# Scores of the first attention stage as float32 products of unsplit keys and queries

## The chip, the cores and the metric

The kernel runs on one core of a Trainium2 chip. TensorE (PE) multiplies, VectorE (DVE), ScalarE (ACT) and GpSimd (POOL) do the elementwise work, SyncE (SP) issues nearly all of the loads. The metric is the device time of one execution in microseconds (us). Before the change, three runs gave 691.86 (median), 690.34 and 691.96 us.

## The reference

Three blocks in a row, all in float32:

```
attention: B=2, H=8, S=768, D=64; key k is kept for query i if k < n_global (8) or 0 <= i-k < n_local (96)
  scores = q k^T / 8 - slope_h * distance;  softmax over the kept keys;  times v
swiglu (1536 tokens x 512): xn = rmsnorm(x);  (silu(xn w_gate) * (xn w_val)) w_out,  inner width 1536
top-1 of 8 experts: y = gate * relu(xe w1[e]) w2[e],  512 -> 1024 -> 512
```

## The kernel before, in words

The 1536 tokens are cut into six **stages** of two 128-row tiles (`SIZES`). A stage's attention is done for four **pairs** of heads (`hp`), so there are 24 groups, numbered `gi` = 4 * stage + pair, of two **units** each (one 128-row tile of queries). Below, (g, t) is unit t of group g; groups 0 to 3 are stage 0, and (4, 0) is the first unit of stage 1.

A unit goes through `scores` (PE products into two PSUM banks, one a head; then on DVE one instruction per head that adds the bias table and takes the row extreme, L492; then the exponential on ACT, L496), `turn` (four PE transposes, L507, copied out by ACT, L515) and `values` (PE products with v, L536; on DVE a reciprocal and the normalised rows into the tiles `part`, L543 to L546). These run up to three units apart. After the last pair of a stage, `tail` normalises its rows (L360 to L374), turns them (L381), and the stage's swiglu products can start (L704, tile `pg`).

PE's products run in the 4-byte format fp32r. The kernel splits their operands in an fp32r copy (the high part) and the rest that the copy leaves out. For the scores, the loads (L202) put a head's 64 dimensions twice on the 128 rows; `prep` makes the high part of the keys on ACT (L429), replaces the lower 64 rows by the rest (L432), makes the high part of the queries (L437 on DVE in the first four groups, L441 on ACT later) and their rest on DVE (L442). One head of a unit is then two fp32r products over 128 rows (L485). For the windowed stages, POOL copies the 32 global keys (`kg`) and the rows of neighbouring tiles into `kt` and `vx` (`pcopy`, L399).

SP loads the first three pairs into tiles of `part` ahead of everything else, five loads a pair (two halves of the keys, two of the queries, one for v). Only then it reads the flag that selects the fast path, and issues the first three swiglu weight loads (`raw`, 512 KB each, L295) and the next pairs. Weights arrive as pairs of words that DVE converts (tile `cv`, L310 to L319). A scheduler sets the order on each engine from the dependencies and its own time model; each engine then runs its list in order, so an instruction that waits holds up all that stand behind it.

Of the kernel before, what the change touches and what calls it, by code (L numbers as in the profile page):

```python
# [8 lines left out]
F32 = mybir.dt.float32  # L9
# [4 lines left out]
ACTF = mybir.ActivationFunctionType  # L14
ALU = mybir.AluOpType
# [4 lines left out]
P = 128  # L20
B, H, S, D = 2, 8, 768, 64
# [3 lines left out]
NP = H // 2  # L25
TT = NT // P
# [19 lines left out]
def kernel(  # L46
# [15 lines left out]
):  # L62
    nc = tc.nc
    slope = [2.0 ** (-(h + 1)) for h in range(H)]
    NFP, LATE = 3, 8
    XT = "ccccss"
    RING = "ccceewweec"
    FIRST = [0, 1, 1, 1, 1]
# [49 lines left out]
        out=nval, in0=nneg, scalar=4294967296.0, in1=nf[:, :, 0], op0=ALU.mult, op1=ALU.add  # L118
# [66 lines left out]
    qT = [q[b].rearrange("h d s -> (h d) s") for b in range(B)]  # L185
# [4 lines left out]
    def rows_of(vn):  # L190
        n = vn.shape[1] // VW
        return vn[:, 0:n * VW].rearrange("p (t c) -> p t c", c=VW)

    def load_pair(st, hp, kn, qn, vn):
# [4 lines left out]
        hd = slice(P * hp, P * (hp + 1))  # L199
        for x, src in ((kn[:, 0:2 * nk * P], kT[b][hd, k0:k0 + nk * P]), (qn[:, 0:2 * nt * P], qT[b][hd, t0 * P:(t0 + nt) * P])):  # L200
# [62 lines left out]
    def body(is_fast):  # L263
# [126 lines left out]

        def fast_attention(pool):
            kg = pool.tile([P, NP, 2, GW], F32R, name="kg")
            vg = pool.tile([P, P], F32, name="vg")
            groups = []
            loaded = list(first_pairs)

            def pcopy(o, i):
                src_ = i.bitcast(F32) if i.dtype == F32R else i
                nc.gpsimd.tensor_scalar(out=o, in0=src_, scalar1=1.0, scalar2=0.0, op0=ALU.mult, op1=ALU.add)  # L399

            def prep(gi):
# [3 lines left out]
                n = nt * P  # L405
                kn, qn, vn = loaded.pop(0)
                vn = rows_of(vn)
                nc.gpsimd.memset(vn[:, i0:nt + 1, 0:VW:VW - 1], 1.0)
                nxt = range(NFP, NFP + 2) if gi == 0 else range(gi + 2, gi + 3) if gi >= NFP else ()
                for gn in nxt:  # L410
                    if gn >= len(order):
# [34 lines left out]
                gr = slice(GW * hp, GW * (hp + 1))  # L446
                if t0 == 0:
                    pcopy(kg[:, hp], kt[:, :, OW + 1, 0:GW])
                    pcopy(vg[gr, :], vn[0:GW, 1, 1:P + 1])

                f = 1 if t0 >= 2 else 3 - t0
                nw = nt + 1 - f
                if nw > 0:
                    pcopy(kt[:, :, f - 1:nt, GW:], kt[:, :, OW + f - 1:OW + nt, GW:])
                    pcopy(kt[:, :, f - 1:nt, 0:GW], kg[:, hp].unsqueeze(2).to_broadcast([P, 2, nw, GW]))
                    pcopy(vx[:, f - 1:nt, :], vn[:, f - 1:nt, :])
                    pcopy(vx[0:GW, f - 1:nt, 1:P + 1], vg[gr, :].unsqueeze(1).to_broadcast([GW, nw, P]))
                mx = pool.tile([P, ST, 2], F32, tag="mx", bufs=3, name="mx")
# [4 lines left out]
            def scores(g, t):  # L463
# [12 lines left out]
                for j, a in ((0, 0), (0, 1), (1, 0), (1, 1)):  # L476
# [81 lines left out]
            n = hold = 0  # L558
# [740 lines left out]
```

## Time and profile before

| what | value |
|---|---|
| runs, median (lowest to highest) | 691.86 us (690.34 to 691.96) |
| profiled execution: own time / span | 690.83 / 689.1 us |
| mean granted TensorE clock | 0.953 of full |
| busy: PE, DVE, ACT, POOL | 637.0, 456.8, 324.6, 338.6 us |
| PE weight loads busy | 574.1 us |
| first score product / first swiglu product | 12.01 / 76.54 us |
| last score product | 168.8 us |

The profiled execution is about 1 us below the median of the runs. PE is busy for 92% of the span, but not evenly: the page's 40 slices show the granted clock at 6, 7 and 5 tenths in the second to fourth slice (17 to 69 us), where attention alone runs, and at 9 nearly everywhere later. From 76.5 us on swiglu products fill the gaps. After attention has ended, the rest is long chains of products. Fp32r shows as f32 in PE's rows.

### The profile page before, as it was taken

Reading aid. Unit: us, or ns where it says so; the run is one execution under the profiler, and the core shown is the slowest. Engines: PE = TensorE matmul, PEld = TensorE weight load, DVE = VectorE, ACT = ScalarE, POOL = GpSimd, SP = SyncE. Lnnn points to the kernel's source line nnn. Section 1 sums busy time; section 2 is a strip of 40 time slices with the busy share of each in tenths; the row PEclk is TensorE's granted clock in tenths of the full one; section 3 lists DMA queues with packets and bytes.
Section 4 is the critical chain, followed back from the end, with each engine's and each line's share of the span. In section 5 each row is a group of like instructions: output and inputs, shape, how many; then the busy total and the mean of one; then the engine's idle time right before and its main releaser. Section 6 shows DMA issues by size and latency. Waiting matters only on the chain. (4 is left out here: it accounts for less than half of the span.)

```text
span 689.1 us, 11953 instructions
## 1 busy us (share of the span) xinstructions
PE 637.0 (92%) x4214; PEld 574.1 (83%) x4215; DVE 456.8 (66%) x1276; ACT 324.6 (47%) x631; POOL 338.6 (49%) x355
## 2 busy tenths in 40 slices
PE   6888998899998899999989999899989899999992
PEld 3677987899997788999889999797678798998891
DVE  6788799987589998225549999952356444555410
ACT  3685777867554543113632211241455545564420
POOL 2577547663254554113332332552777677667401
PEclk9675899999999999999999999999999999999997
DMA  6977447641034444000440120131578776667200
GB/s 182 235 193 185 107 127 180 176 132 35 1 119 125 127 130 145 1 1 6 163 138 14 50 62 32 49 120 63 167 241 242 192 251 206 201 195 228 82 12 28
DMA packets 57290, 85.16 MB, mean 124 GB/s; under 512 B 6655, under 2 KB 39423, under 8 KB 57216
## 3 DMA queue, kind: packets, MB, share of 16 engines
q1 hardware_dynamic: 54272, 76.91, 38.5%
q0 software_dynamic: 2944, 7.35, 3.2%
q8 instruction: 36, 0.59, 0.4%
q14 instruction: 38, 0.31, 0.2%
HBM read 77.91 MB, written 7.39 MB: 124 GB/s over the span
## 5 line engine op out<-in xcount | busy, mean ns | idle before, releaser
L704 PE MATMUL pg<-xn,gv 128*128 128x256 f32 x1728 | 229.0, 286 | 7.0 <-DVE hf L717 3.6
L704 PEld LDWEIGHTS pg<-xn,gv 128*128 128x128 f32 x1728 | 219.1, 192 | 13.8 <-DVE hf L717 4.9
L891 POOL TENSOR_TENSOR ew<-rawe,ew 128x512 fp32r<-128x512 f32 x64 | 100.8, 1590 | 48.2 <-ACT ew L885 46.4
L722 POOL TENSOR_TENSOR hid<-hf,hid 128x256 fp32r<-128x256 f32 x72 | 59.0, 824 | 119.9 <-ACT hid L721 119.6
L741 PE MATMUL po<-ow,hid 128*128 128x512 f32 x432 | 112.2, 399 | 1.5 <-DVE hf L717 1.2
L888 DVE TENSOR_TENSOR ew<-rawe,ew 128x512 fp32r<-128x512 f32 x64 | 65.4, 1027 | 68.2 <-ACT ew L885 67.5
L885 ACT ACTIVATE ew<-rawe 128x1024 fp32r<-128x1024 f32 x64 | 66.7, 1060 | 65.8 <-DMA rawe<-in_moe_w_dram 53.8
L945 PE MATMUL py<-ew,eh 128*128 128x512 f32 x384 | 91.2, 395 | 0.9 <-DVE eh L1012 0.9
L741 PEld LDWEIGHTS po<-ow,hid 128*128 128x128 f32 x432 | 77.4, 189 | 17.4 <-POOL hid L722 1.5
L967 PE MATMUL ph<-xs,ew 128*128 128x256 f32 x672 | 84.0, 283 | 3.6 <-ACT yo L951 2.7
L945 PEld LDWEIGHTS py<-ew,eh 128*128 128x128 f32 x384 | 71.4, 188 | 17.6 <-DVE eh L1012 1.5
L967 PEld LDWEIGHTS ph<-xs,ew 128*128 128x128 f32 x672 | 81.7, 189 | 4.9 <-ACT yo L951 2.9
L721 ACT ACTIVATE hid<-hf 128x256 fp32r<-128x256 f32 x72 | 29.8, 415 | 82.3 <-DVE hf L717 82.2
L774 DVE CUSTOM_DVE_ANT_0 jk<-part,rgb 128x256 bf16<-128x256 f32 x128 | 59.4, 507 | 0.0
L485 PE MATMUL sp<-kt,qt 128*128 128x256 f32 (+1 forms) x192 | 47.2, 351 | 12.0 <-DVE mx L492 5.6
L496 ACT ACTIVATE pr<-pr,mx 128x256 f32<-128x256 f32 (+1 forms) x96 | 44.5, 484 | 19.5 <-DVE mx L492 17.8
L327 POOL TENSOR_TENSOR gv<-cv,gv 128x512 fp32r<-128x512 f32 x24 | 32.8, 1370 | 34.4 <-ACT gv L326 31.8
L485 PEld LDWEIGHTS sp<-kt,qt 128*128 128x128 f32 x192 | 34.2, 227 | 18.0 <-DVE mx L492 5.8
L712 ACT ACTIVATE th<-pg 128x256 f32<-128x256 f32 x72 | 26.8, 376 | 44.1 <-PE pg L704 42.7
L713 DVE SCALAR_TENSOR_TENSOR th<-th,pg 128x256 f32<-128x256 f32 x72 | 29.6, 414 | 26.8 <-ACT th L712 26.8
L432 POOL TENSOR_TENSOR kt<-kn,kt 64x768 fp32r<-64x768 f32 (+1 forms) x21 | 38.0, 1811 | 8.8 <-issue 4.0
L316 DVE SCALAR_TENSOR_TENSOR cv<-raw,cv 128x512 uint32<-128x512 uint32 x36 | 35.8, 997 | 0.5
(174 smaller groups left out, 898.2 us busy)
## 6 DMA issues: line engine op xcount, KB each, us to landing
rawe<-in_moe_w_dram SPq DMA_DIRECT2D x64, 512.0 KB, 4.1
raw<-in_moe_w_gate_dram SPq DMA_DIRECT2D x12, 512.0 KB, 4.1
raw<-in_moe_w_val_dram SPq DMA_DIRECT2D x12, 512.0 KB, 3.7
raw<-in_moe_w_out_dram SPq DMA_DIRECT2D x12, 512.0 KB, 3.6
kn<-in_k_dram SPq DMA_DIRECT2D x32, 192.0 KB, 3.6
qn<-in_q_dram SPq DMA_DIRECT2D x42, 128.0 KB, 3.5
vn<-in_v_dram SPq DMA_DIRECT2D x16, 192.0 KB, 3.0
x1d<-part SPq DMA_DIRECT2D x12, 256.0 KB, 2.1
```

The source lines that it names most:

```text
L432: lo_eng[kq[0]].tensor_tensor(out=ks[D:P], in0=src[D:P], in1=ks[D:P].bitcast(F32), op=ALU.subtract)
L485: mm = nc.tensor.matmul(out=o, lhsT=qt[:, j, a, t * P:(t + 1) * P], rhs=rhs, start=(a == 0), stop=(a == 1))
L496: pin["act"] = nc.scalar.activation(out=pr[:, j, 0:n], in_=pr[:, j, 0:n], func=ACTF.Exp, bias=mx[:, t, j:j + 1], scale=-1.0,)
L704: nc.tensor.matmul(out=pg[:, 0:n_], lhsT=gv[:, i, a, kk, :], rhs=x[st][:, kk, :], start=(n == 0), stop=(n == 3 * KD - 1),)
L722: nc.gpsimd.tensor_tensor(out=hh[:, 1], in0=hf, in1=hh[:, 0].bitcast(F32), op=ALU.subtract)
L741: nc.tensor.matmul(out=po, lhsT=hid[mi][:, a, t * P:(t + 1) * P], rhs=ow[:, c, :], start=(mi == 0 and n == 0), stop=(mi == len(ms) - 1 and ...
L774: nc.vector.tensor_tensor_reduce(out=jk, in0=part[i0 + t][:, h * 256:(h + 1) * 256], in1=rgb[h][:, e, :], scale=1.0, scalar=0.0, op0=ALU.m ...
L885: cp = nc.scalar.activation(out=t[:, 0], in_=raw, func=ACTF.Copy)
L888: nc.vector.tensor_tensor(out=t[:, 1, 0:NDV], in0=raw[:, 0:NDV], in1=t[:, 0, 0:NDV].bitcast(F32), op=ALU.subtract)
L891: nc.gpsimd.tensor_tensor(out=t[:, 1, NDV:], in0=raw[:, NDV:], in1=t[:, 0, NDV:].bitcast(F32), op=ALU.subtract)
L945: last_mm["py"] = nc.tensor.matmul(out=py, lhsT=hid(m, a, j), rhs=w2t[m // 2][:, c, (m % 2) * DM:(m % 2 + 1) * DM], start=(n == 0), stop=( ...
L967: nc.tensor.matmul(out=ph[:, 0:CAP], lhsT=w1t[kk][:, a, m * P:(m + 1) * P], rhs=x[:, kk, :], start=(n == 0), stop=(n == 3 * KD - 1),)
```

## The change

For groups below `NRAWG` = 4, that is all four pairs of stage 0, keys and queries are loaded once: head 0 on rows 0 to 63, head 1 on rows 64 to 127. ACT scales the queries in place, and one head of a unit is one float32 product over its 64 rows. Four pairs instead of three are loaded ahead (`NFP`), three loads each, in two tiles of `part`. The ones beside v are set before the loads. As no split keys of stage 0 exist any more, the global keys come by two extra loads (`kgn`, 128-byte pieces), and ACT and POOL split them at group 2.

```diff
-    NFP, LATE = 3, 8
+    NFP, LATE = 4, 8
+    NRAWG = 4
...
+        if is_raw(st, hp):
+            nc.sync.dma_start(out=kn[:, 0:nk * P], in_=kT[b][hd, k0:k0 + nk * P])
+            nc.sync.dma_start(out=qn[:, 0:nt * P], in_=qT[b][hd, t0 * P:(t0 + nt) * P])
+            nc.sync.dma_start(out=rows_of(vn)[:, i0:i0 + nk, 1:P + 1], ...)
+            return kn, qn, vn
...
-    first_pairs = [load_pair(*order[i], *part[TT - 3 * (i + 1):TT - 3 * i]) for i in range(NFP)]
+    for i in range(NFP):
+        kq_, vn_ = part[TT - 2 * i - 2], part[TT - 2 * i - 1]
+        nc.gpsimd.memset(rows_of(vn_)[:, 1:3, 0:VW:VW - 1], 1.0)
+        first_pairs.append(load_pair(*order[i], kq_[:, 0:STAGE], kq_[:, STAGE:2 * STAGE], vn_))
...
+                if gi == 0:
+                    kg0 = kT[0].rearrange("(h d) s -> d h s", d=D)[:, :, 0:GW]
+                    for r in range(2):
+                        nc.sync.dma_start(out=kgn[D * r:D * (r + 1)].rearrange("d a j s -> d (a j) s"), in_=kg0)
+                if gi == 2:
+                    nc.scalar.activation(out=kg, in_=kgn, func=ACTF.Copy)
+                    nc.gpsimd.tensor_tensor(out=kg[D:P], in0=kgn[D:P], in1=kg[D:P].bitcast(F32), op=ALU.subtract)
...
+                if raw_:
+                    qs = qn[:, 0:n]
+                    nc.scalar.activation(out=qs, in_=qs, func=ACTF.Copy, scale=0.125 / slope[2 * hp])
+                    values_windows()
+                    groups.append((st, t0, hp, qs, (kn, kgr), vn, vx, mx))
+                    return
...
+                    for j in range(2):
+                        r = slice(D * j, D * (j + 1))
+                        lq = qt[r, t * P:(t + 1) * P]
+                        if t0 == 0:
+                            mm = nc.tensor.matmul(out=sp[j][:, 0:n], lhsT=lq, rhs=kn[r, 0:n], start=True, stop=True)
```

The scheduler makes new lists. On ACT, the first instructions behind the branch were the high keys of pairs 0, 1 and 2 (`part_120`, `part_117`, `part_114`):

```order
L429 ACTIVATE kt<-part_120 128x2x256
L429 ACTIVATE kt<-part_117 128x2x256
L496 ACTIVATE pr<-pr,mx 128x128 x2
L429 ACTIVATE kt<-part_114 128x2x256
L496 ACTIVATE pr<-pr,mx 128x256
```

Now they are the scalings of the queries of pairs 1, 2, 3 and, last, 0 (`part_119`, `part_117`, `part_115`, `part_121`):

```order
L470 ACTIVATE part_119<-part_119 128x256
L470 ACTIVATE part_117<-part_117 128x256
L470 ACTIVATE part_115<-part_115 128x256
L470 ACTIVATE part_121<-part_121 128x256
L558 ACTIVATE pr<-pr,mx 128x128 x2
L558 ACTIVATE pr<-pr,mx 128x256
L483 ACTIVATE kt<-kn 128x2x384
```

Pair 0's queries stand behind the last loaded pair's. On DVE, the row extremes of unit (1, 0) (`tab_145`, `half_165`) and of unit (1, 1) (`tabL`, `half_167`) had one weight conversion between them, and the queries of pair 3 (`qn`) behind them:

```order
L492 ISA pr,mx<-sp,tab_145 128x128
L492 ISA mx 128x1
L492 ISA pr,mx<-sp,half_165 128x128
L492 ISA mx 128x1
L310 TENSOR_SCALAR cv<-cv 128x512
L313 TENSOR_SCALAR cv<-cv 128x512
L316 SCALAR_TENSOR_TENSOR cv<-raw,cv 128x512
L492 ISA pr,mx<-sp,tabL 128x256
L492 ISA mx 128x1
L492 ISA pr,mx<-sp,half_167 128x256
L492 ISA mx 128x1
L437 TENSOR_SCALAR qt<-qn 128x2x256
```

Now, from the second head of (1, 0) on (`half_166`), the rests of the queries of pairs 4 and 5 (L496) stand there:

```order
L554 ISA pr,mx<-sp,half_166 128x128
L554 ISA mx 128x1
L496 SCALAR_TENSOR_TENSOR qt<-qn,qt 128x2x256
L333 SCALAR_TENSOR_TENSOR cv<-raw,cv 128x512
L554 ISA pr,mx<-sp,tabL 128x256
L554 ISA mx 128x1
L336 SCALAR_TENSOR_TENSOR cv<-raw,cv 128x512
L496 SCALAR_TENSOR_TENSOR qt<-qn,qt 128x2x256
L554 ISA pr,mx<-sp,half_168 128x256
L554 ISA mx 128x1
```

Both heads of (1, 1) now stand behind a load of a later stage. On SP, the list behind the branch is now this; before, pair 3 stood where pair 4 (the first `kn`, `qn`, `vn`) stands now, and pair 4 where pair 5 stands, with the weights all three ahead of them:

```order
L312 DMA raw<-in_moe_w_gate_dram 128x4x256
L312 DMA raw<-in_moe_w_val_dram 128x4x256
L215 DMA kn<-in_k_dram 64x2x384
L312 DMA raw<-in_moe_w_out_dram 128x1024
L215 DMA kn<-in_k_dram 64x2x384
L215 DMA qn<-in_q_dram 64x2x256 x2
L219 DMA vn<-in_v_dram 128x3x128
L215 DMA kn<-in_k_dram 64x2x384 x2
L215 DMA qn<-in_q_dram 64x2x256
L235 DMA gB<-in_moe_rms_g_dram 128x512
L215 DMA qn<-in_q_dram 64x2x256
L219 DMA vn<-in_v_dram 128x3x128
```

Pair 5's loads moved forward, the `kgn` loads follow two and five places behind. The first swiglu product stands behind the same number of units as before on PE (60 transposes and 56 value products in either list).

## Rows read from the trace of the kernel before

**Rows 1.** Windows: stretch; length, busy us (count) of PE, PEld, DVE, ACT, POOL; clock, DMA, GB/s

```profile
24.00:42.00 18.00, 16.27 (x68) 13.94 (x67) 14.26 (x46) 12.93 (x28) 14.12 (x16) 0.53 0.81 198
42.00:51.00 9.00, 6.49 (x52) 5.68 (x50) 8.77 (x29) 7.76 (x17) 6.54 (x9) 1.00 0.83 218
51.00:74.50 23.50, 19.63 (x85) 17.96 (x86) 18.62 (x55) 13.72 (x28) 17.06 (x22) 0.51 0.69 171
74.50:170.00 95.50, 89.39 (x702) 84.88 (x702) 85.80 (x287) 74.27 (x163) 54.99 (x83) 0.98 0.47 128
170.00:560.00 390.00, 371.78 (x2492) 336.79 (x2492) 260.27 (x717) 150.56 (x286) 173.64 (x158) 0.99 0.33 103
```

**Rows 2.** Timeline of PE: start, us, what, count, idle time before and its releaser

```profile
12.01 0.66 PE L485 MATMUL sp<-kt,qt 128*128 128x128 f32 x4 [2.10 <-DVE kt L432]
...
33.37 0.80 PE L485 MATMUL sp<-kt,qt 128*128 128x256 f32 x2 [0.91 <-POOL kt L399]
...
51.21 1.11 PE L485 MATMUL sp<-kt,qt 128*128 128x256 f32 x4 [1.51 <-POOL kt L399]
...
76.54 0.61 PE L704 MATMUL pg<-xn,gv 128*128 128x256 f32 x3
...
77.58 1.91 PE L704 MATMUL pg<-xn,gv 128*128 128x256 f32 x14
```

**Rows 3.** Timeline of SP's queue: start, us of issuing, load, count

```profile
1.77 1.37 SPq L202 DMA_DIRECT2D part<-in_k_dram  x2
...
10.94 0.59 SPq L206 DMA_DIRECT2D part<-in_v_dram  x1
12.61 0.38 SPq L295 DMA_DIRECT2D raw<-in_moe_w_gate_dram  x1
...
22.33 0.60 SPq L206 DMA_DIRECT2D vn<-in_v_dram  x1
```

**Rows 4.** DMA view, 0 to 14 us: load, count, KB each, median us to landing

```profile
part<-in_q_dram SPq DMA_DIRECT2D x6, 128.0 KB, 3.0
```

**Rows 5.** Timeline of DVE up to the first unit of stage 1

```profile
4.88 0.17 DVE L112 CAST nf<-nraw 128x4 f32<-128x4 int32 x1 [2.33 <-DMA nraw<-in_n_local_dram]
...
10.55 0.69 DVE L442 SCALAR_TENSOR_TENSOR qt<-part,qt 128x512 fp32r<-128x512 f32 x1
11.27 0.69 DVE L432 TENSOR_TENSOR kt<-part,kt 64x512 fp32r<-64x512 f32 x1
...
19.93 0.42 DVE L492 CUSTOM_DVE_ANT_0 pr<-sp,half 128x256 f32<-128x256 f32 x1
...
22.23 0.43 DVE L437 TENSOR_SCALAR qt<-qn 128x512 fp32r<-128x512 f32 x1 [1.87 <-DMA qn<-in_q_dram]
...
34.20 0.42 DVE L492 CUSTOM_DVE_ANT_0 pr<-sp,tabG 128x256 f32<-128x256 f32 x1 [0.31 <-PE sp L485]
```

**Rows 6.** Timelines of ACT and, below it, of POOL

```profile
9.02 0.29 ACT L257 ACTIVATE half<-tab 128x128 f32<-128x128 f32 x1
9.44 1.15 ACT L429 ACTIVATE kt<-part 128x512 fp32r<-128x512 f32 x2
...
26.65 0.63 ACT L441 ACTIVATE qt<-qn 128x512 fp32r<-128x512 f32 x1 [0.53 <-DMA qn<-in_q_dram]
...
15.99 1.69 POOL L432 TENSOR_TENSOR kt<-part,kt 64x512 fp32r<-64x512 f32 x1 [0.60 <-POOL kg L399]
...
35.16 2.16 POOL L432 TENSOR_TENSOR kt<-kn,kt 64x768 fp32r<-64x768 f32 x1
```

**Rows 7.** One tile's forms, PE, 52 to 74 us: count: ns min/median/max, first and last start

```profile
L485 PE MATMUL sp<-kt,qt x18: 415/415/583, 51.7 to 71.8; 128*128 128x256 f32 x18
...
L536 PE MATMUL xp<-vn,ptS x20: 417/417/418, 54.4 to 73.4; 128*128 128x65 f32 x20
```

**Rows 8.** DMA view, 12 to 26 us: load, count, KB each, median us to landing

```profile
qn<-in_q_dram SPq DMA_DIRECT2D x4, 128.0 KB, 5.9
...
rg<-in_moe_w_gate_dram SPq DMA_DIRECT2D x1, 16.0 KB, 5.6
```

More of the change, by code (lines that the diff above doesn't have):

```diff
@@ L192, in rows_of, with is_raw @@
         return vn[:, 0:n * VW].rearrange("p (t c) -> p t c", c=VW)
+    def is_raw(st, hp):
+        return st * NP + hp < NRAWG
     def load_pair(st, hp, kn, qn, vn):
@@ L392, in fast_attention @@
             kg = pool.tile([P, NP, 2, GW], F32R, name="kg")
+            kgr = pool.tile([P, NP, GW], F32, name="kgr") if NRAWG > NP else None
+            kgn = pool.tile([P, NP, 2, GW], F32, name="kgn")
             vg = pool.tile([P, P], F32, name="vg")
@@ L407, in prep @@
                 vn = rows_of(vn)
-                nc.gpsimd.memset(vn[:, i0:nt + 1, 0:VW:VW - 1], 1.0)
+                raw_ = is_raw(st, hp)
+                if gi >= NFP:
+                    nc.gpsimd.memset(vn[:, i0:nt + 1, 0:VW:VW - 1], 1.0)
                 nxt = range(NFP, NFP + 2) if gi == 0 else range(gi + 2, gi + 3) if gi >= NFP else ()
@@ L417, in prep, with values_windows @@
                 nk = nt + 1 - i0
+                if gi == 0:
+                    kg0 = kT[0].rearrange("(h d) s -> d h s", d=D)[:, :, 0:GW]
+                    for r in range(2):
+                        nc.sync.dma_start(
+                            out=kgn[D * r:D * (r + 1)].rearrange("d a j s -> d (a j) s"), in_=kg0
+                        )
+                    if kgr is not None:
+                        nc.sync.dma_start(out=kgr, in_=kT[0].rearrange("(a p) s -> p a s", p=P)[:, :, 0:GW])
+                if gi == 2:
+                    nc.scalar.activation(out=kg, in_=kgn, func=ACTF.Copy)
+                    nc.gpsimd.tensor_tensor(
+                        out=kg[D:P], in0=kgn[D:P], in1=kg[D:P].bitcast(F32), op=ALU.subtract
+                    )
+                OW = ST_MAX
+                gr = slice(GW * hp, GW * (hp + 1))
+                f = 1 if t0 >= 2 else 3 - t0
+                nw = nt + 1 - f
+                vx = pool.tile([P, 3, VW], F32, tag="vx", bufs=2, name="vx")
+                mx = pool.tile([P, ST, 2], F32, tag="mx", bufs=3, name="mx")
+                def values_windows():
+                    if t0 == 0:
+                        pcopy(vg[gr, :], vn[0:GW, 1, 1:P + 1])
+                    if nw > 0:
+                        pcopy(vx[:, f - 1:nt, :], vn[:, f - 1:nt, :])
+                        pcopy(vx[0:GW, f - 1:nt, 1:P + 1], vg[gr, :].unsqueeze(1).to_broadcast([GW, nw, P]))
+                if raw_:
[4 more added lines that the diff above has]
+                    return
                 qt = pool.tile([P, 2, 2, STAGE], F32R, tag="qt", bufs=2, name="qt")
                 kt = pool.tile([P, 2, 2 * ST_MAX + 1, P], F32R, tag="kt", bufs=2, name="kt")
-                OW = ST_MAX
-                vx = pool.tile([P, 3, VW], F32, tag="vx", bufs=2, name="vx")
                 src = kn[:, 0:2 * nk * P].rearrange("p (j t n) -> p j t n", j=2, t=nk)
@@ L445, in prep @@
                 )
-                gr = slice(GW * hp, GW * (hp + 1))
                 if t0 == 0:
                     pcopy(kg[:, hp], kt[:, :, OW + 1, 0:GW])
-                    pcopy(vg[gr, :], vn[0:GW, 1, 1:P + 1])
-                f = 1 if t0 >= 2 else 3 - t0
-                nw = nt + 1 - f
                 if nw > 0:
@@ L475, in scores @@
                 OW = ST_MAX
-                for j, a in ((0, 0), (0, 1), (1, 0), (1, 1)):
+                raw_ = is_raw(st, hp)
+                if raw_:
+                    kn, kgr_ = kt
+                    for j in range(2):
+                        r = slice(D * j, D * (j + 1))
+                        lq = qt[r, t * P:(t + 1) * P]
+                        if t0 == 0:
+                            mm = nc.tensor.matmul(
+                                out=sp[j][:, 0:n], lhsT=lq, rhs=kn[r, 0:n], start=True, stop=True
+                            )
+                        else:
+                            nc.tensor.matmul(out=sp[j][:, 0:GW], lhsT=lq, rhs=kgr_[r, hp, :], start=True, stop=True)
+                            mm = nc.tensor.matmul(
+                                out=sp[j][:, GW:n], lhsT=lq, rhs=kn[r, t * P + GW:(t + 2) * P], start=True, stop=True
+                            )
+                for j, a in () if raw_ else ((0, 0), (0, 1), (1, 0), (1, 1)):
                     o = sp[j][:, 0:n]
```

9 lines of the change are left out of this document (6 added, 3 removed).

## The prediction, made before the changed kernel ran

> **What bounds the kernel now.** I read the page first, then windows, then the timelines of the first 80 us. The windows [rows 1] show three regimes. From 74.5 us on PE is the bound: 89.4 of 95.5 us busy until 170 and 371.8 of 390 until 560, at nearly the full clock. Nothing after 170 us depends on attention. Before 74.5 us no engine is full. From 24 to 42 us PE, DVE, ACT and POOL are busy 16.3, 14.3, 12.9 and 14.1 of 18 us, from 51 to 74.5 us PE 19.6, DVE 18.6 and POOL 17.1 of 23.5, and in both stretches the clock is 0.51 to 0.53, the 1.2 GHz level. It is 1.00 from 42 to 51 us. This is a chain of in-order engines that wait for one another. So the change is worth what it moves the first swiglu product, at 76.54 us [rows 2]: behind it PE takes its work without a hole worth speaking of, and I carry a shift there to the end one to one. All terms below are shifts of that instant, counted against the profiled execution's 690.83 us, which is 1.03 under the median 691.86; a shift is taken off either.
>
> **The loads.** SP issues 15 loads ahead of the branch from 1.77 to 10.94 us, 0.655 us apart, and the first weight load follows the last of them by 1.67 us, at 12.61 [rows 3]. Twelve loads end with an issue at 1.77 + 11 x 0.655 = 8.98, so the weights go at 10.65: 1.96 us earlier.
>
> **The start.** This does not move. The first score product ran at 12.01, released by DVE's rest of the keys [rows 2]. Now it waits for the scaled queries of pair 0, which ACT does last, behind those of pair 3. These are the 11th load, issued at 1.77 + 10 x 0.655 = 8.3; with 3.0 us to landing [rows 4] they are there at 11.3. Two scalings at about 0.3 each (ACT took 0.29 for 128x128, and two of 128x512 took 1.15 [rows 6]) give 11.9. ACT is free from 9.3 on, so the wait costs nothing else. The four sets of ones, now ahead of the tables on POOL, stand before work for which DVE waits on the load of `n_local` anyway, until 4.88 us [rows 5]; nothing.
>
> **The work that goes.** On DVE: four high parts of queries (0.43), four rests of queries (0.69) and two rests of keys (0.69): 1.72 + 2.76 + 1.38 = 5.9 us [rows 5]. On POOL: two rests of keys, 1.7 each [rows 6], and four small copies, less one rest of the global keys (64x256, half of the 1.7): about -3. On ACT: four high keys (1.15 for two: 2.3) against four scalings and one kg copy (five at 0.3 to 0.4): -0.5.
>
> **PE's products.** A 65-column float32 product takes 417 ns at the low clock, a 256-column fp32r one 415 [rows 7]: a float32 column costs like four. At the full clock 14 products of 256 columns took 1.91 us, 0.136 each [rows 2]. A head of a 256-column unit was two of these (0.27) and is now one of four times the price (0.55): +0.27. With four such units and four of 128 columns, two heads each, 8 x 0.27 + 8 x 0.14 = +3.3 us at the full clock, +6.5 at the low one. No row shows two products on separate halves of the rows: the other end of the range is that they run side by side, 0. I take the upper end, since every neighbouring row on PE shows products one after another; but only what PE does after 26 us can be late for anybody, three of the eight units, and there DVE needs as long (below): it costs 0.5 us.
>
> The Trainium skill, TensorEngine Tiling (Array Packing), Key Properties, says that different row tiles can load and multiply in parallel. No run here shows it; by that rule the 3.3 us would be 0 and my 0.5 would go. The same list says that a change of tiling mode drains the engine, which no row here shows either.
>
> **Where the work comes back: two waits on DVE and ACT.** In the new DVE list the rests of the queries of pairs 4 and 5 stand ahead of the row extremes of unit (1, 1). Those need loads that before came later. From the first weight load (12.61) until pair 4's last queries were used (26.65, ACT waiting for that load [rows 3, 6]) 14.0 us passed and 3.12 MB were asked for: three weights 1.57, pair 3 0.65, pair 4's keys 0.39 and queries 0.26, the row gB 0.26. That is 0.223 MB a us. Up to pair 5's last queries the new list asks for weights 1.57, pair 4 0.85, pair 5's keys and queries 0.65 and gB 0.26: 3.33 MB, 14.9 us, from 10.65 on: 25.6. ACT's high part (0.63) and DVE's rest (0.69) follow, so the second row extreme of (1, 1) starts at 27.0, against 19.93 before [rows 5]. Behind it stand DVE's conversions and the row extremes of groups 2 and 3, all of whose data is there: 8 row extremes 2.9, conversions 3.8, normalising 1.5, sum 8.2. The first of (4, 0) then starts at 35.7, against 34.20 [rows 5]; with the 0.5 of PE at 36.2: +2.0 us. Before, the same queue had waited 1.87 for pair 3's queries [rows 5], so a wait of this sort is replaced, not invented. ACT also waits, for the global keys kgn, issued behind pair 5; I take 26 to 27 us, hidden beside the wait for pair 5.
>
> The skill's DMA: Bandwidth & Descriptors, Specifications, asks for at least 512 bytes a piece for full rate. kgn's pieces are 128 bytes. The trace has 32-byte pieces (rg) in the same stretch, landed after 5.6 us, no later than the 5.9 of the large loads beside it [rows 8], so I price it at nothing; by the rule its wait on ACT would outlast pair 5's by some us.
>
> **What stage 1 gains.** At (4, 0) before, only pair 4 was prepared; now pair 5 is too. POOL is thereby ahead by a rest of keys (2.16 [rows 6]) and its window copies. PE waited 0.91 and 1.51 us for such copies, at 33.37 and 51.21 [rows 2]: -2.4. DVE has one rest of queries (0.69) and half a conversion (0.5) less to do up to the first swiglu product: -1.2. The clock was low until 42 us, and again from 51, where PE had just waited for POOL [rows 1, 2]. With float32 products PE has fewer holes from 28 us on, and I take it that the rise comes some us sooner. In 24 to 42 us PE did 16.3 us of work at half speed; a few us of it at full speed are worth half of themselves, of which PE, the fullest of four, keeps perhaps half: -0.9.
>
> **Sum.** +2.0 - 2.4 - 1.2 - 0.9 = -2.5 us: the first swiglu product at about 74.0 and 691.86 - 2.5 = 689.4 us.
>
> **Rivals.**
> *It only repays itself.* The two waits of PE for POOL become waits of PE for DVE, which is busy 8.8 of 9 us in 42 to 51 [rows 1]. Then of the gains only 1.2 to 2 remain, against +2.0: 691.9, between 690 and 693.5. For it: no engine has more than a quarter free. Against: PE is what is fullest at the low clock, and POOL's copies are what it waits for.
> *Slower: the queue behind pair 5.* If pair 5's last queries land after about 27.5 us, or the kgn split reaches POOL after 30, unit (1, 1) and all behind it start late, PE idles from 18 to 27, falls to the low clock, and does float32 products there at four times the columns: 6.5 us x 3/4 of them not hidden, 4.9 instead of my 0.5. (4, 0) comes at 40, and stage 1 gives back 2.4 + 1.2 only: +2.5 to +5, say 695.3. For it: the DMA engines are saturated there, and the load behind which DVE now waits is one pair later. Against: fewer bytes are asked for before, and they start 2 us sooner.
> *The clock stays up.* If POOL's lead removes the gap at 50 us, PE stays at 2.4 GHz through 51 to 74.5. Its 19.6 us of busy time there would halve, DVE's 18.6 would bound the stretch: 23.5 - 18.6 = 4.9 less, with the 1.2 and part of the rest 6 us: 685.9. For it: 42 to 51 us went at the full clock with PE only 6.5 of 9 us busy. Against: the low clock came back after one gap, and many can make one.
> That the change doesn't do what it says is excluded by the lists: the split of stage 0 is gone from them.
>
> **Chances.** My forecast 0.34, the clock staying up 0.13, repaying itself 0.29, the queue behind pair 5 0.24. About 0.3%, 2.1 us, is what a measurement of this kernel can tell from no change. Below 689.8 lie the clock's case and most of the forecast's own spread (with a tenth of the repaid one): 0.47. Within: 0.30. Above 693.9: 0.23. The range for 8 in 10 reaches from 684.8 to 694.8; the forecast's own is 687 to 691.
>
> **What would show it.** First weight load near 10.65 us; first score product near 12; a hole on DVE before unit (1, 1) until about 26 us; the first `tabG` row extreme near 36; the first swiglu product near 74; PE's waits for POOL copies in stage 1 smaller; clock 1.00 again before 40 us. I am wrong if (4, 0) comes before 34 us (the loads were faster than counted), if it comes at 39 or later (the slower rival), or if the first swiglu product moves and the end doesn't.

## The result, and the profile after

The changed kernel is slower: 700.62 us (median of 4 runs, 698.28 to 704.0) against 691.87 (median of 4), a ratio of 1.0123 with a 95% interval of 1.0087 to 1.016, so +8.75 us. Medians here and below are of all runs of a kernel, ratios leave out single runs in a slower state (one or two each in e5, e7, e8, e9, e13 and e20). The profiled execution took 704.0 us (span 702.3), the longest of the four and 3.4 above the median; that of before was 1 below its own. The traces therefore differ by 13.2 us, more than the medians. In windows, with the columns of [rows 1]:

```profile
12.00:24.00 12.00, 7.11 (x23) 2.91 (x21) 1.49 (x11) 3.10 (x7) 0.92 (x1) 0.64 0.94 226
24.00:42.00 18.00, 18.00 (x57) 11.45 (x57) 11.68 (x33) 10.08 (x22) 11.04 (x15) 0.50 0.66 163
42.00:51.00 9.00, 9.00 (x38) 7.51 (x38) 6.50 (x25) 5.05 (x11) 1.59 (x3) 0.50 0.20 59
51.00:74.50 23.50, 19.57 (x103) 17.66 (x101) 22.92 (x65) 17.68 (x37) 15.93 (x18) 0.64 0.58 165
74.50:170.00 95.50, 87.50 (x645) 83.25 (x646) 85.27 (x262) 68.48 (x152) 59.78 (x84) 0.91 0.49 137
```

Two things are new. From 12 to 24 us DVE works for 1.49 us and POOL for 0.92: they wait. From 24 to 51 us PE shows no idle time at all, at a granted clock of 0.50, which is 1.2 GHz; before, it had 16.27 of 18 us at 0.53 and then 6.49 of 9 at 1.00 [rows 1]. What DVE and POOL wait for stands on ACT. Its timeline, with the issues of SP's queue below it:

```profile
14.85 0.51 ACT L558 ACTIVATE pr<-pr,mx 128x256 f32<-128x256 f32 x1 [1.99 <-DVE mx L554]
22.10 0.84 ACT L483 ACTIVATE kt<-kn 128x768 fp32r<-128x768 f32 x1 [6.74 <-DMA qn<-in_q_dram]
22.85 0.49 ACT L558 ACTIVATE pr<-pr,mx 128x256 f32<-128x256 f32 x1
...
8.61 0.39 SPq L312 DMA_DIRECT2D raw<-in_moe_w_gate_dram  x1
9.09 0.45 SPq L312 DMA_DIRECT2D raw<-in_moe_w_val_dram  x1
9.59 0.73 SPq L215 DMA_DIRECT2D kn<-in_k_dram  x1
10.37 1.15 SPq L312 DMA_DIRECT2D raw<-in_moe_w_out_dram  x1
11.56 0.82 SPq L215 DMA_DIRECT2D kn<-in_k_dram  x1
...
23.84 0.60 SPq L443 DMA_DIRECT2D kgn<-in_k_dram  x1
```

The high keys of pair 4 (L483) stand between the two exponentials of unit (0, 1). Their two loads are issued among and behind the three weights, and ACT stands still for 6.74 us (the view names another load, `qn`; what the instruction reads is `kn`). The second exponential, the weight conversions and all turns of later units wait behind it. PE and DVE show the rest (DVE's three rows at the end):

```profile
11.01 0.80 PE L530 MATMUL sp<-part 64*128 64x128 f32 x4 [1.44 <-ACT part L470]
...
23.40 0.69 PE L569 MATMUL pp<-ident,pr 128*128 128x128 f32 x2 [4.89 <-ACT pr L558]
24.01 1.22 PE L530 MATMUL sp<-part 64*128 64x256 f32 x2
...
34.16 1.22 PE L530 MATMUL sp<-part 64*128 64x256 f32 x2
...
42.86 1.22 PE L530 MATMUL sp<-part 64*128 64x256 f32 x4
...
45.20 0.77 PE L547 MATMUL sp<-kt,qt 128*128 128x256 f32 x2
...
85.15 0.60 PE L766 MATMUL pg<-xn,gv 128*128 128x256 f32 x3
...
30.40 0.41 DVE L554 CUSTOM_DVE_ANT_0 pr<-sp,half 128x256 f32<-128x256 f32 x1
...
37.82 0.42 DVE L554 CUSTOM_DVE_ANT_0 pr<-sp,half 128x256 f32<-128x256 f32 x1 [1.37 <-PE sp L530]
...
46.01 0.42 DVE L554 CUSTOM_DVE_ANT_0 pr<-sp,tabG 128x256 f32<-128x256 f32 x1 [0.52 <-PE sp L547]
```

After a hole of 4.89 us PE needs from 24.01 to 45.20, 21.2 us, to reach unit (4, 0), and now DVE waits for PE. The first row extreme of (4, 0) is at 46.01 (34.20 before [rows 5]), the first swiglu product at 85.15 (76.54 [rows 2]). A float32 head leaves two records; one alone takes 1.22 us at 1.2 GHz (34.16, x2), and so do both heads of a unit when they stand together (42.86, x4).

**Where the time is.** PE's busy time in each 2-us window of the whole span, times the granted clock there, is its work at full clock; the rest of the busy time is lost to the low clock; what remains is idle. The three add up to the span:

| profiled execution | span | work | lost to low clock | idle |
|---|---|---|---|---|
| before | 689.1 | 612.8 | 24.2 | 52.1 |
| after | 702.3 | 613.2 | 36.3 | 52.8 |

Of 13.2 us, 12.1 are TensorE's time at 1.2 GHz, 0.7 idle, 0.4 work. That is an account, not yet a cause, and it is that of the longest execution: in e9, where the same load stands at the same place on ACT, the wait was 4.86 us. The two suspects are the waits on loads (theory A) and the price of the float32 products (theory B).

### The profile page after: what moved, and what is told of

The parts are those of the page before. It is cut to its first block, busy times and chain, and to the rows that moved or that the text cites. A ratio compares the mean times of both kernels' runs of the same rounds, so it can differ in the third digit from the quotient of the medians.

```text
span 702.3 us, 11931 instructions
## 1 busy us (share of the span) xinstructions
PE 649.5 (92%) x4214; PEld 579.2 (82%) x4215; DVE 461.3 (66%) x1266; ACT 323.5 (46%) x632; POOL 335.1 (48%) x350
## 3 DMA queue, kind: packets, MB, share of 16 engines
q1 hardware_dynamic: 54176, 75.99, 36.2%
## 5 line engine op out<-in xcount | busy, mean ns | idle before, releaser
L953 POOL TENSOR_TENSOR ew<-rawe,ew 128x512 fp32r<-128x512 f32 x64 | 98.8, 1558 | 48.4 <-ACT ew L947 48.0
L803 PE MATMUL po<-ow,hid 128*128 128x512 f32 x432 | 113.7, 403 | 1.5 <-DVE hf L779 1.2
L950 DVE TENSOR_TENSOR ew<-rawe,ew 128x512 fp32r<-128x512 f32 x64 | 68.9, 1082 | 64.8 <-ACT ew L947 62.8
L803 PEld LDWEIGHTS po<-ow,hid 128*128 128x128 f32 x432 | 78.9, 193 | 17.9 <-POOL hid L784 1.4
L558 ACT ACTIVATE pr<-pr,mx 128x256 f32<-128x256 f32 (+1 forms) x96 | 44.5, 485 | 25.4 <-DVE mx L554 23.4
L486 POOL TENSOR_TENSOR kt<-kn,kt 64x768 fp32r<-64x768 f32 (+1 forms) x20 | 36.6, 1831 | 19.1 <-ACT kt L483 12.4
L547 PE MATMUL sp<-kt,qt 128*128 128x256 f32 (+1 forms) x160 | 38.0, 341 | 5.6 <-DVE mx L554 3.7
L569 PE MATMUL pp<-ident,pr 128*128 128x128 f32 x176 | 36.8, 319 | 4.9 <-ACT pr L558 4.9
L779 DVE SCALAR_TENSOR_TENSOR hf<-th,pg 128x256 f32<-128x256 f32 x72 | 29.7, 414 | 9.7 <-PE pg L766 8.0
```

Source lines behind the costliest of these rows:

```text
L547: mm = nc.tensor.matmul(out=o, lhsT=qt[:, j, a, t * P:(t + 1) * P], rhs=rhs, start=(a == 0), stop=(a == 1))
L558: pin["act"] = nc.scalar.activation(out=pr[:, j, 0:n], in_=pr[:, j, 0:n], func=ACTF.Exp, bias=mx[:, t, j:j + 1], scale=-1.0,)
L569: nc.tensor.transpose(pp[:, (j * nb + a) * P:(j * nb + a + 1) * P], pr[:, j, a * P:(a + 1) * P], ident)
L803: nc.tensor.matmul(out=po, lhsT=hid[mi][:, a, t * P:(t + 1) * P], rhs=ow[:, c, :], start=(mi == 0 and n == 0), stop=(mi == len(ms) - 1 and ...
L950: nc.vector.tensor_tensor(out=t[:, 1, 0:NDV], in0=raw[:, 0:NDV], in1=t[:, 0, 0:NDV].bitcast(F32), op=ALU.subtract)
L953: nc.gpsimd.tensor_tensor(out=t[:, 1, NDV:], in0=raw[:, NDV:], in1=t[:, 0, NDV:].bitcast(F32), op=ALU.subtract)
```

## The experiments

Each was timed beside the kernel before on its chip, which was not the same for all; the medians of before lie between 690.0 and 691.9 us, so ratios compare better across rows than medians. The ratio is to it, with its 95% interval; the last two columns are the account above, each of one profiled execution, whose own time is given too (in e9, e15 and e20 it lies 4 to 5 us under the median and in e3 4.5 above, so there the account is that of a better or a worse execution).

| run | median us | ratio | profiled | low clock | idle |
|---|---|---|---|---|---|
| after | 700.6 | 1.0123 (1.0087 to 1.016) | 704.0 | 36.3 | 52.8 |
| e1 pair 4, 5 behind | 701.1 | 1.0148 (1.0108 to 1.0188) | 702.0 | 25.4 | 59.4 |
| e2 cheap products | 692.6 | 1.0015 (0.999 to 1.0039) | 692.2 | 23.5 | 55.8 |
| e3 = e1 and e2 | 689.6 | 0.9965 (0.9939 to 0.9992) | 694.2 | 29.5 | 54.2 |
| e4 weights later | 697.7 | 1.0095 (1.0065 to 1.0125) | 697.8 | 28.3 | 53.3 |
| e5 no load waits | 690.7 | 0.9995 (0.9958 to 1.0032) | 689.4 | 14.2 | 57.0 |
| e6 = e5, heads together | 690.8 | 0.9991 (0.9963 to 1.0019) | 689.9 | 22.0 | 53.1 |
| e7 = e5 and e2 | 696.2 | 1.0062 (1.0036 to 1.0089) | 693.6 | 19.7 | 60.1 |
| e8 before, products twice | 697.0 | 1.0078 (1.005 to 1.0107) | 696.3 | 18.1 | 60.4 |
| e9 hole filled | 699.9 | 1.0115 (1.0081 to 1.0148) | 695.0 | 19.2 | 55.6 |
| e10 kgn first | 688.3 | 0.9937 (0.991 to 0.9963) | 689.3 | 22.1 | 50.4 |
| e12 = e5, warm start | 690.5 | 0.9978 (0.9956 to 1.0) | 690.5 | 14.8 | 58.0 |
| e13 pair 4 and kgn first | 694.0 | 0.9991 (0.9955 to 1.0028) | 694.1 | 31.8 | 49.0 |
| e15 = e9, warm start | 698.3 | 1.0126 (1.0097 to 1.0155) | 693.8 | 23.4 | 51.9 |
| e16 = e10, warm start | 692.0 | 1.0025 (1.0008 to 1.0041) | 692.7 | 25.5 | 52.1 |
| e17 keys one step later | 706.2 | 1.0234 (1.0201 to 1.0266) | 705.3 | 35.8 | 52.8 |
| e20 = e17, warm start | 704.0 | 1.0168 (1.0119 to 1.0218) | 699.7 | 25.8 | 57.9 |
| e21 warm start alone | 695.9 | 1.0082 (1.0052 to 1.0112) | 695.6 | 25.7 | 54.2 |

**Waits or price.** The first four kernels.

```diff
 # e1: in prep, for pairs 4 and 5; exps = last exponential of each unit
+if gi in (4, 5): behind(high keys on ACT, exps[3 if gi == 4 else 5])   # and the high queries
 # e2: top(x) = upper 16 bits of x, read in place as bfloat16
-out=sp[j][:, 0:n], lhsT=lq,      rhs=kn[r, 0:n],      start=True
+out=sp[j][:, 0:n], lhsT=top(lq), rhs=top(kn[r, 0:n]), start=True
 # e3: both.  e4: in load64, for the first three weights
+behind(weight load, load of pair 4's v)
```

> The changed kernel, with ACT's high keys and queries of pairs 4 and 5 put behind the exponentials of units (1, 1) and (2, 1) in its list, so that no exponential of stage 0 stands behind a load that lands late. Nothing else is changed. Theory A (the loss is ACT's in-order wait on pair 4's keys, 15.4 to 22.1 us, and PE's hole of 4.9 us that follows): PE's hole shrinks to under 2 us, the first row extreme of (4, 0) comes at 40 to 41.5 instead of 46.0, the first swiglu product at 79 to 81, and the time falls by 5 to 7, to 694 to 696. Theory B (the loss is PE's own work, float32 products at the low clock): the hole goes but PE stays busy without a break and (4, 0) comes at 43 or later; time 698 to 700.

> The changed kernel with the score products of stage 0 on the upper 16 bits of keys and queries, read in place as bfloat16 (the lower 16 bits of both are left out): the same products, rows and columns, at a quarter of the passes or less. Nothing is loaded or prepared in another way. Theory A (ACT's wait alone): ACT still waits for pair 4's keys until about 22, PE's hole stays, (4, 0) moves by under 1.5 us, time 699 to 701. Theory B (PE's float32 work at the low clock is what fills 24 to 45 us): a head costs 0.4 instead of 1.22 us, PE has holes after 26 us, (4, 0) comes at 41 or earlier, time 694 to 696; if the granted clock also rises before 45 us, 692 to 694.

> Both edits of the two runs before: pair 4 and 5 behind the exponentials on ACT, and score products of stage 0 on the upper 16 bits (the lower 16 bits are left out). If A and B are two terms that follow each other (a hole of 4.9, then PE-bound work of 21.8 us), they add: (4, 0) at 34 to 37, time 689 to 692. If they hide each other, this is no better than the better of the two: 694 to 696.

> The changed kernel with the first three weight loads issued behind pair 4's five loads instead of among them. The scheduler then puts pair 4's high keys ahead of the first exponential on ACT. Theory A: pair 4's keys land 3 to 5 us after an issue at about 8.6, so at 12.5 to 14, ACT waits 1 to 2 us instead of 6.74, and the time falls by 3 to 5 to 695.5 to 697.5, less whatever the weights lose that come 2.5 us later. Theory B: no change, 699 to 701.

e1 gained nothing, but it did not test what it was made for. ACT in e1, and PE's hole:

```profile
27.87 0.42 ACT L450 ACTIVATE kg<-kgn 128x256 fp32r<-128x256 f32 x1 [7.41 <-DMA kgn<-in_k_dram]
...
29.01 0.69 PE L575 MATMUL pp<-ident,pr 128*128 128x128 f32 x2 [5.31 <-ACT pr L563]
```

With pair 4's keys out of the way the next late load, kgn, stopped ACT even longer, and again PE had a hole. e2 brought nearly everything back (8.1 us), as theory B said, though ACT still waited 4.07 us for pair 4's keys. But it is no clean test of the price either. Its list on ACT differs from the changed kernel's: the keys stand behind the second exponential of (0, 1), the first weight and the first copy of transposes (`ptS`), no longer between the exponentials:

```profile
15.35 0.36 ACT L580 ACTIVATE ptS<-pp 128x256 f32<-128x256 f32 x1
19.79 0.85 ACT L486 ACTIVATE kt<-kn 128x768 fp32r<-128x768 f32 x1 [4.07 <-DMA kn<-in_k_dram]
```

e3 brought 11.0, so e1's edit, worth nothing alone, was worth 3.0 on top of e2. e4 gained 2.9, but its interval overlaps that of the changed kernel.

**All load waits gone.**

```diff
 # e5 = e1, and in prep(0) kgn's two loads are issued first;
+behind(first three weight loads and the loads of pairs 4 and 5, last load of kgn)
 # e6 = e5, and in turn() and values(), while stage 0's scores are being emitted
+behind(transpose or value product, second head's score product of the newest unit)
 # e7 = e5 with e2's products.  e8: kernel before, stage 0 only
-for j, a in ((0, 0), (0, 1), (1, 0), (1, 1)):
+for j, a in [(j, a) for j in range(2) for a in (0, 1, 0, 1)]:
```

> The first experiment again (pairs 4 and 5 behind the exponentials on ACT), and kgn's two loads issued right behind the first twelve, ahead of the weights: in the first experiment ACT had only exchanged the wait for pair 4's keys for one of 7.41 us for kgn, until 27.87. Now no instruction of ACT in stage 0 stands behind a load that lands after 14 us but the first weight conversion. Theory A (waits on loads are the loss): no hole of PE over 2 us before 40, (4, 0) at 34 to 37, first swiglu product at 75 to 78, time 690 to 692. Theory B (PE's own work at the low clock is the loss): PE busy without a hole, (4, 0) at 38 to 41, first swiglu product at 79 to 82, time 694 to 698.

> The run before it (no load waits), and on PE the two score products of a unit of stage 0 stand one behind the other: transposes and value products of older units are put behind the second head. In the changed kernel's trace a unit whose heads stand together took 1.22 us at the low clock (42.86 us, four records), and each head alone took 1.22 as well (34.16 and 36.57, two records each). If the heads run side by side on their two halves of the rows, a 256-column unit costs 1.22 instead of 2.44 us and PE has some 4 us less to do up to (4, 0): (4, 0) 2 to 4 us earlier than in the run before it, time 2 to 4 less. If those four records were only short by chance, a unit stays at 2.4 and the time within 1 us or worse, since PE now waits for the second bank.

> No load waits, and score products of stage 0 on the upper 16 bits (the lower 16 bits of keys and queries are left out). Theory B: against the run with float32 products and the same loads 5 to 8 us less, 687 to 690. Theory A: within 2 us of it.

> The kernel before, with every score product of stage 0 done twice into the same bank (both passes, then both again; the second result replaces the first). Loads, preparation and all other work are as before. A unit's head then costs about 1.5 instead of 0.78 us at the low clock, more than the 1.22 of a float32 head: some 9 us more PE work over stage 0. Theory B: PE's price alone makes a loss of the size seen, 4 to 8 us: 696 to 700. Theory A (PE has room in stage 0, only waits cost): under 2 us, 691 to 694.

e5 is theory A's number: 690.7, with every product still float32. Its windows, and on PE the first products of units (1, 1) and (4, 0):

```profile
12.00:24.00 12.00, 12.00 (x55) 6.54 (x54) 6.42 (x28) 7.92 (x18) 2.77 (x6) 0.83 1.09 270
24.00:42.00 18.00, 15.35 (x88) 12.30 (x89) 17.39 (x48) 12.89 (x28) 12.70 (x14) 0.81 0.69 180
...
18.71 0.70 PE L542 MATMUL sp<-part 64*128 64x256 f32 x2
...
28.72 0.70 PE L542 MATMUL sp<-part 64*128 64x256 f32 x4
...
31.15 1.09 PE L559 MATMUL sp<-kt,qt 128*128 128x256 f32 x4 [1.14 <-POOL kt L427]
```

The way from (1, 1) to (4, 0), 21.2 us after the change, is 12.4 here: the same products, at a clock that was 1.00 from 16 to 32 us. So theory B is wrong as a cause by itself, and theory A alone explains too little: ACT waited 6.74 us, and (4, 0) moved by 11.8. My reading is that while PE is full and the clock is low, everything PE does there counts twice; cheaper products (e2, with its other list) or a clock that stays up (e5) each remove that, and with one of them the other has nothing left to give. It doesn't hold for every run. e1 is as slow as the changed kernel with hardly more low clock than before (25.4 against 24.2 us): its loss is 7.3 us more idle time and 2.6 more work. e7 agrees only in so far as cheaper products on top of e5 gained nothing: they were 5.5 us slower, not 5 to 8 faster. In its list PE waited 4.22 us for POOL before (4, 0), and the clock was 0.50 from 51 to 74.5 us. e8 lost 5.3 with twice the products, but its list also moved: ACT waited 4.07 us for keys (23.21) and PE 6.48 for POOL, so it doesn't price the products. e6 shows the heads side by side (unit (1, 1) at the low clock, both heads):

```profile
19.72 1.22 PE L543 MATMUL sp<-part 64*128 64x256 f32 x4
```

PE's work over the span was 3.4 us less than in e5 (613.1 against 616.5), as expected; the time was the same, since 7.8 more were lost to the low clock and 3.9 less idle.

**What keeps the clock down.** Warm products are PE products whose result nobody reads; the kernel has some of its own. (Six of them stand in the 21.2 us after the change and take 2.6 us there, by their starts and those of the next rows; no run left them out.) Theory C is that the wait costs twice: as a hole, and then by the low clock into which the hole leads.

```diff
 # e9: 17 more warm products behind unit (1, 0)'s scores, PE's work that waits for ACT behind them
 # e10: kgn first, as in e5, and no pins on ACT.  e13: kgn and pair 4 first, then the weights
 # e12: e5, and behind(first score product, 10th warm product of WARM1)   # 5 stood ahead of it
```

> The changed kernel with 17 more warm products (128 rows by 512 bfloat16 columns, results unused) on PE between unit (1, 0)'s scores and the work that waits for ACT's stall: ACT still waits for pair 4's keys until about 22, but PE's hole of 4.9 us is filled with products whose result nobody reads. Theory C (the wait costs twice: once as a hole, and then because PE falls to the 1.2 GHz level in the hole and does its float32 products there): the granted clock stays at 1.00 behind the hole, the 21.8 us from 23.4 to 45.2 shrink to 13 to 16, (4, 0) at 37 to 40, time 692 to 695. Theory D (the clock is low there because of the float32 products themselves, not because of the hole): the clock is back at 0.50 within a few us, (4, 0) at 44 or later, time 699 to 703.

> The changed kernel with kgn's two loads first behind the twelve, and nothing put behind anything on ACT: pair 4's keys stand where the scheduler puts them, ahead of the exponentials of unit (1, 0), and land at 20 to 22. Theory C: ACT waits 3 to 5 us there, PE has a hole of 2 to 4 us, falls to the low clock before 24 and stays there through the float32 products: (4, 0) at 39 to 43, time 695 to 698, between the run without load waits (690.7) and the changed kernel (700.6). If only kgn mattered, it equals 690.7.

> The changed kernel with another order of the loads and nothing else: kgn and pair 4 go first behind the twelve, the three weight loads behind them; no instruction is pinned on ACT, the scheduler makes the lists. Theory C: ACT's waits for loads in stage 0 are down to 1 or 2 us each (pair 4 lands at 13 to 15), PE has no hole over 2 us before 30, (4, 0) at 34 to 37, time 689 to 692. If the weights that land 2.5 us later are waited for instead, 693 to 696.

> The kernel without load waits (690.7), and five more of its warm products moved ahead of the first score product, so that PE does not stand idle from 9.8 to 11.0 us, where the granted clock fell to 0.50 until 16. Theory C: the clock is 1.00 from 10 us on and the first units come 1 to 2 us earlier; what reaches the first swiglu product is 0 to 2 us: 688.5 to 691. If the clock falls with the float32 products whatever stands ahead of them, 690 to 692 and 0.50 again until 16.

e9 failed: of 24 warm products in a row (18.28 to 24.8) the first ran at the low clock, they ended 4 us behind ACT's wait (20.25), PE then had a new hole of 2.59 us, and from 32 to 48 us it was busy for all 16 us at 0.50. e12 did what it should: the clock was 1.00 from 10 to 30 us, through all float32 products, and its 12 runs lie between 688.5 and 693.0, where those in e5's ratio lie between 686.0 and 695.2. The median did not move: behind the float32 products PE waited 5.81 us for POOL's keys (at 32.33), and the account shows 58.0 us idle. e10 was the surprise: one change of the order of loads, 688.3, 12.3 us under the changed kernel and faster than before (0.9937, 0.991 to 0.9963). It still had a wait of ACT and a hole, both shorter:

```profile
20.46 0.84 ACT L490 ACTIVATE kt<-kn 128x768 fp32r<-128x768 f32 x1 [3.81 <-DMA kn<-in_k_dram]
...
22.41 0.33 PE L576 MATMUL pp<-ident,pr 128*128 128x128 f32 x1 [2.57 <-ACT pr L565]
```

With kgn early, the scheduler put pair 4's keys behind both exponentials of (0, 1). (4, 0) came as late as 41.58 in this run. e13 has almost no wait for a load on ACT (2.34 at most), yet 26 us at the low clock (18 to 44) and 31.8 in the account: 694.0.

**Wait or clock.** Five kernels to part the two.

```diff
 # e15: e9 and e12's warm start, pair 4's keys pinned between the heads of (0, 1).  e16: e10, warm start
 # e17: if gi == 4: behind(high keys on ACT, exps[1])    # and nothing else
 # e20: e17, warm start.  e21: pair 4's keys pinned as in e15, warm start, nothing added
```

> The changed kernel with ACT's wait for pair 4's keys kept at its place (between the two heads of unit (0, 1)), five warm products moved ahead of the first score product, and 20 more (results unused) on PE where it waited for ACT. In the run that filled the hole without a warm start, the clock was 0.50 until 20 us and the filling products themselves ran at it, until 26. Theory C (the loss is PE's time at 1.2 GHz, into which the hole leads): clock 1.00 from 10 us through the hole, PE's work of 24 to 45 us done in 12 to 16, (4, 0) at 36 to 40, time at the low clock up to the last score product under 20 us (31.6 in the changed kernel), time 690 to 694. Theory A (the wait itself): ACT, DVE and POOL lose the same 6 us whatever PE does: 698 to 701.

> The changed kernel with one edit: ACT's high keys of pair 4 may not stand ahead of the second exponential of unit (0, 1). Now they stand behind it and the first weight's absolute values, one place later; loads as in the changed kernel, kgn late. Theory C: PE gets the transposes of (0, 1) 7 us earlier, the hole moves to the value products of (0, 0) and is 2 to 4 us instead of 4.9, as in the run with kgn first (2.57): time 690 to 696. If kgn's position was what mattered there: 698 to 701.

> kgn's loads first (688.3 by itself) and five warm products moved ahead of the first score product. Theory C: the clock is 1.00 from 10 us on, the hole behind pair 4's keys stays, time at the low clock up to the last score product under 19 us: 685 to 689. If the start gains nothing, 688; if the list that the scheduler makes of it puts pair 4's keys ahead of more work, 689 to 693.

> The changed kernel, ACT's wait for pair 4's keys kept between the two heads of unit (0, 1), loads as they are, and five of its warm products moved ahead of the first score product. Theory E (time lost is PE's busy time at 1.2 GHz, and the level at the start of the float32 products decides much of it): clock 1.00 from 10 us to ACT's wait, so the first units are done earlier and the hole is longer (5 to 7 us); behind it 0.50 until stage 1, so only the part before the hole is won: (4, 0) at 40 to 43, 693 to 698. Theory A (the wait alone): as the changed kernel, 699 to 702.

> The slowest run (706.2: pair 4's keys behind the second exponential of unit (0, 1)) with five of its warm products moved ahead of the first score product. Theory E: the clock is 1.00 from 10 us until PE waits for ACT (near 17), so that the low stretch is 10 us shorter at its start: (4, 0) at 38 to 41, time 692 to 697. If its list behind the wait is what makes it slow: 702 to 706.

e17 is the strongest case against the wait, and against the hole behind ACT's wait as what keeps the clock low. Its windows:

```profile
12.00:24.00 12.00, 11.16 (x32) 5.16 (x30) 4.94 (x19) 4.64 (x10) 2.12 (x3) 0.50 1.07 254
24.00:42.00 18.00, 18.00 (x58) 11.36 (x59) 9.04 (x32) 9.62 (x22) 8.86 (x13) 0.50 0.57 139
42.00:51.00 9.00, 9.00 (x53) 8.45 (x52) 7.57 (x23) 6.80 (x14) 3.62 (x4) 0.66 0.22 59
```

ACT waits 3.46 and 1.83 us for keys instead of once 6.74, and PE has no hole over 0.84 us between 12 and 50, but the clock is 0.50 from 12 to 48 us without a break (it had fallen before 12, where PE stood idle for 1.35 us ahead of the first score product), and it is the slowest kernel of all, 5.6 us behind the changed one. e21 is the counterpart: ACT's wait is kept, though shorter (4.91 us, until 18.88 instead of 22.10), and the clock at the start is up (0.83 from 12 to 24 us, 0.64 after the change); the low clock costs 25.7 instead of 36.3 us, and the time is 695.9: 4.8 us less by the medians, 2.8 by the ratios, whose intervals overlap. So perhaps a third to a half of the loss goes with the level at the start, not cleanly parted from the shorter wait, and the whole of it where the load waits go as well (e5, e12). That the clock and the time go together shows inside one kernel too, where no list differs: e3's 12 executions reach from 685.3 us at a mean clock of 0.966 to 694.2 at 0.944, and in all 18 kernels of the table the longer executions tend to have the lower clock. e15 and e20 say where this ends: with the clock up from 14 us on in e15 (it was 0.50 from 8 to 14) and from 12 in e20, another wait of ACT in their lists (1.1 to 1.2 us for queries and kgn in e15, 6.28 for pair 4's queries in e20) opened a hole of PE of 2.65 and 5.53 us, and behind it the clock was 0.50 until stage 1 again: 698.3 and 704.0. e16, expected at 685 to 689, shows that the two gains don't add: 692.0.

Still open: why two lists with nearly the same wait on ACT, e10 (3.81) and e17 (3.46), end 18 us apart. One difference is what stands behind the wait. The first copy of transposes is ahead of it in e10 and behind it in e17 (e10 above, e17 below):

```profile
16.29 0.36 ACT L584 ACTIVATE ptS<-pp 128x256 f32<-128x256 f32 x1
...
19.69 0.84 ACT L484 ACTIVATE kt<-kn 128x768 fp32r<-128x768 f32 x1 [3.46 <-DMA kn<-in_k_dram]
20.44 0.36 ACT L581 ACTIVATE ptS<-pp 128x256 f32<-128x256 f32 x1
```

PE's value products, which read the copy, start at 18.33 in e10 and at 20.90 in e17. The runs in which ACT waits more than 2 us for a load of pair 4 sort by it: 688.3 to 692.6 us with the copy ahead of the wait (e2, e10, e16), 695.9 to 706.2 with the copy behind it (the changed kernel, e9, e15, e17, e20, e21). No run moves the copy alone, so this is not shown as a cause. The clock is another difference: in e10 it came back at 16 us for 7 us, in e17 it didn't; I found nothing in the rows before 16 us that explains it. Nor is the clock all: two executions of e17 had mean clocks of 0.950 and 0.949 and took 703.2 and 703.6 us, where e4's six, at 0.942 to 0.953, took 696.9 to 701.3. And e17 takes 527 us from its last score product (at 176.2) to its end, where all other runs but e7 (525) have 519 to 523; I don't know why.

## Why the prediction was wrong, step by step

- **The step that failed is the first term of the sum**, the shift of (4, 0), "+2.0": it was +11.8, since (4, 0) came at 46.01 where I had 36.2. Two parts of it failed. The wait: I followed the rests of queries on DVE and named (1, 1)'s second row extreme, 27.0; it came at 30.40, 3.4 us later, because ACT stood still until 22.10 for pair 4's keys. The overlap: from there to (4, 0) I counted 9.2 us, DVE's time, with PE's products hidden but for 0.5 us; it took 15.6, because PE had no idle time at 1.2 GHz and DVE waited for it.
- **The clock**, the last term, had the wrong sign: "I take it that the rise comes some us sooner", -0.9. It came at 51 us instead of 41, and the low clock took 12.1 us more. The thought behind it, that PE with fewer holes gets its clock back, is what e17 speaks against.
- **PE's products.** My ground for the 0.5 us was that only the work after 26 us can be late for anybody and that DVE needs as long. From unit (1, 1) to (4, 0) PE needed 21.2 us at 1.2 GHz, DVE less (11.68 busy of 18 us in 24 to 42), and nothing of PE's work was hidden. The price itself was smaller than my four times: at 2.4 GHz a float32 head alone takes 0.70 us and both heads of a unit together also 0.70 (e5), where a unit's four fp32r products took 0.72 before:

```profile
19.06 0.72 PE L485 MATMUL sp<-kt,qt 128*128 128x256 f32 x4
```

  So a unit costs as much as before when its heads stand together, and twice that when they don't. I took "products one after another" from the neighbouring rows, which was right for heads that stand apart only. The Trainium skill's page TensorEngine Tiling (Array Packing), Key Properties, says that different tiles can multiply in parallel. The rows at 42.86, in e5 and in e6 agree (1.22, 0.70 and 1.22 us for both heads).
- **The loads.** The first weight load came at 8.61, not 10.65 (twelve issues from 1.77 to 7.16, 0.49 us apart, not 0.655). That was not the gain I took it for: the list puts the three weights, 1.57 MB, ahead of the second half of pair 4's keys. The first score product came at 11.01, not near 12.
- **Where the work comes back.** The wait that mattered stood in the ACT list that I had shown, one row below the first exponential of (0, 1). For kgn I wrote "26 to 27 us, hidden"; it was hidden only as long as pair 4's keys were late too (e1). Kgn was late since it was issued at 23.84; its two loads of 64 KB landed 2.4 us after their issue, qn's of 128 KB after 5.4 (medians up to 30 us). The Trainium skill's page DMA: Bandwidth & Descriptors, Specifications, asks for at least 512 bytes a piece for full rate. kgn's pieces are 128 bytes; no run here tests the rule, since kgn's loads are also smaller than the others.
- **Stage 1** gained what I said, in part by luck: from (4, 0) to the first swiglu product 39.1 instead of 42.3 us, -3.2 against -3.6 without the clock. PE's waits for POOL are gone there, but others for DVE came in their place: PE's idle time in the stretch fell only from 6.4 to 5.4 us, and the other 2.2 are less busy time, which I hadn't counted.
- **The carrying to the end.** The first swiglu product moved by 8.6 us, the medians by 8.75, but from it to the end of the span the runs need 609 to 621 us. The last score product is the better mark (row starts 168.6 before, 180.1 after; 519 to 523 us to the end in all runs but e7 and e17). (4, 0) is a worse one: 41.58 in e10 with 688.3 us, 33.16 in e12 with 690.5.
- **The rivals.** The slower one ("queue behind pair 5") had the right chain, a load wait, an idle PE from 18, the low clock, float32 products at it, and its price was too small: (4, 0) at 40 instead of 46. The load that it named was not the one: ACT stood for pair 4's keys, not for pair 5's queries. It got 0.24 since I argued from bytes that loads start sooner.
- **The run nearest to the forecast** is e5: (4, 0) at 35.2 and the first swiglu product at 74.1, where I had 36.2 and 74.0, and 690.7 us for my 689.4, though its ratio, 0.9995, shows no gain over before. What the sum missed is what the order of the lists does to the waits and to the level of the clock.

## What to carry to other kernels

Where a change moves loads, go through every in-order list for the first instruction that reads each moved load, and ask what stands behind it; take away one such wait and look for the next. Where an engine is near its limit and its clock can halve, cost a change at both levels: work that is hidden at the full clock may be paid, and doubled, at the low one. A small load that many lists need is worth trying first: here it brought the whole loss back (e10). And since each edit makes the scheduler write new lists, compare the lists before a run is read as a test of one thing (e2).

## What the runs showed of the hardware that I had not expected

- The granted clock can stay at 0.50 for 26 us (after, 24 to 50) and 36 us (e17, 12 to 48) in which PE's rows show almost no idle time, and stay at 1.00 through such float32 products in other lists (e5 from 16 to 32, e12 from 10 to 30). That they begin at 1.00 isn't enough: in e13 it was back near 1.00 from 14 to 18 us (0.88 and 0.97) and fell to 0.50 after two holes of PE of 0.85 and 0.95 us. In the runs that were low from 28 us on, and have float32 products, it rose 1 to 7 us after the first row extreme of unit (4, 0).
- Two 64-row float32 products of the two halves, one behind the other, take 1.22 us at 1.2 GHz and 0.70 at 2.4, as one does alone.
- One execution of the same program can differ by 9 us from another (e5, 686.0 to 695.2); with five products more ahead of its first one the 12 executions of e12 lie within 4.5.
